# First DFT stage of batches 2 to 7: sums and differences of mirrored rows on GpSimd, 14 products of 120x120 in place of 16 of 94x96

## The chip, the cores and the metric

The kernel runs on one core of a Trainium2 chip. The metric is the device time of one execution in microseconds, the median of several runs. The engines are called TensorE (PE; PEld is its loading of weights), VectorE (DVE), ScalarE (ACT), GpSimd (POOL) and SyncE (SP), as the profile does.

## What is computed

An input x of shape (8, 3008, 256) is filtered along its sequence in the frequency domain, and the result goes through a feed-forward layer with a snake activation:

```python
X = np.fft.rfft(x, axis=1)
y = np.fft.irfft(X * (filt_r + 1j * filt_i)[None], n=3008, axis=1)
x = y.reshape(8 * 3008, 256)
h = x @ w_in                            # 256 -> 2048
g = h + np.sin(alpha * h) ** 2 / (alpha + 1e-09)
out = g @ w_out                         # 2048 -> 256
```

## The kernel before

The sequence of 3008 is split as 47 x 64: position t = 64 n1 + n2. The forward transform of a batch has a **first stage** over n1 (47 rows to 24 frequencies s, real and imaginary parts), a second stage over n2 with the twiddle factors in its tables, a product with the filter, and two stages back. The class `Spectral` holds a batch; batch 0 is done by code of its own before the main loop, and batch 1 shares its methods with batches 2 to 7.

- `load_x` (line 141) brings one of four chunks of x from DRAM as fp16, by a casting DMA that GpSimd issues: 94 partitions (47 n1 by two halves h of the 64 columns n2), 8 columns n2 of 256 channels each. For batches from 2 on it waits for the latest snake operation issued so far, which paces it.
- `first` (line 181) is the first stage: 16 matrix products per batch of the table `wf_t` (94x96) with two columns n2, so 512 columns on TensorE, into a PSUM tile `pa`. `evac` (lines 160 and 162) copies each to `t1_h`, two times in three on ACT and once on DVE. After every fourth product a DMA on SP stores the finished eight columns to `d1` in DRAM (line 186).
- `load_t2` (line 193, DMAs of GpSimd) reads `d1` back with n2 on the partitions. `forward` (line 201) is the second stage; its result `xf` is copied by ACT, and SP sends it back with its two halves exchanged as `xs` (line 208). `product` (line 215) and `cross` (lines 221 and 222) are three products or sums on DVE, each with both inputs in SBUF. `inverse` (line 232) and `last` (line 254) go back to `y` in SBUF.
- The feed-forward layer runs over 48 chunks of up to 512 tokens. `hidden` makes 16 blocks per chunk: two products into one of four PSUM buffers `ph` (line 540), the sine on ACT (`cos_all`, line 544), and one DVE operation that reads `cos_all` and `ph` and writes `v` (line 545), called the snake here. `project` (line 557) multiplies the chunk before by `w_out`.

The order of the work is written out by hand. The main loop counts **steps**, eight per chunk, 48 per batch; a step issues two `hidden` blocks and a part of `project`. `put(at, ...)` lists a piece of the spectral work with the step at which it is due, and `slot` issues what is due between them, at most one piece on TensorE at a time. With z = 48 b for batch b, its x is loaded from z - 92 on, the first stage starts at z - 67, `load_t2` is due at z - 56, the second stage runs from z - 46.8 and the last stage ends in the steps after z. Batch 2 has due times of its own: loads at steps 22, 27, 32 and 37, the first stage from step 36. So the first stage of a batch overlaps with the filter products of the batch before. All engines execute their instructions in the order in which they were issued. PSUM tiles `pa`, `pb`, `pc` and `pd` share two buffers; x has four buffers.

Of the kernel before, what the change touches and what calls it, by code (L numbers as in the profile page):

```python
# [18 lines left out]
B, S, C = 8, 3008, 256  # L19
DFF = 2048  # L20
N1, N2 = 47, 64
NS, NQ = 24, 64
NR = 2 * N1
NK = 4 * NS
FUSED = 1


def dft_tables():

    n1, n2 = np.arange(N1), np.arange(N2)  # L30
    s, q = np.arange(NS), np.arange(NQ)
    ph = 2 * np.pi * np.outer(n1, s) / N1
    w = np.stack([np.cos(ph), -np.sin(ph)], 1)
    wf = np.zeros((N1, 2, 2, NS, 2))
    wi = np.zeros((2, NS, 2, N1, 2))
    v = np.stack([2 * np.cos(ph), -2 * np.sin(ph)], 0)
    v[0, :, 0], v[1, :, 0] = 1.0, 0.0
    for h in range(2):
        wf[:, h, :, :, h] = w
        wi[:, :, h, :, h] = v.transpose(0, 2, 1) * (8.0 / S)  # L40

    kap = np.where(q[:, None] < 32, s + N1 * q[:, None], s + N1 * (95 - q[:, None]))
# [12 lines left out]
    wi0[:, :, :NS] = wi.transpose(0, 2, 1, 3)  # L55
    d = d.reshape(128, NS, 128).astype(f16)
    e = d.transpose(2, 1, 0) * f16(0.125)
    return (wf.reshape(NR, NK).astype(f16), wi.reshape(NK, NR).astype(f16), d,
            wf0.reshape(96, 128).astype(f16), wi0.reshape(128, NR).astype(f16), e)


# [1 line left out]
def kernel(  # L63
# [8 lines left out]
    out: bass.AP,  # L72
):
    nc = tc.nc
    wf_host, wi_host, d_host, wf0_host, wi0_host, e_host = dft_tables()
    wf_dram = nc.inline_tensor(wf_host, name="wf_tbl")
    wi_dram = nc.inline_tensor(wi_host, name="wi_tbl")
    d_dram = nc.inline_tensor(d_host, name="d_tbl")
    wf0_dram = nc.inline_tensor(wf0_host, name="wf0_tbl")
    wi0_dram = nc.inline_tensor(wi0_host, name="wi0_tbl")  # L80
# [6 lines left out]
    def after(ins, other):  # L87

        tc.add_manual_dep(ins.ins, other.ins.name, mybir.DependencyInfo(
            mybir.DependencyClass.Sync, mybir.DependencyReason.DATA), reason="order of loads")  # L90

    def pool(name, bufs, space=None):
        kw = {} if space is None else {"space": space}
        return ctx.enter_context(tc.tile_pool(name=name, bufs=bufs, **kw))

    cpool = pool("consts", 1)
    xpool = pool("xp", 4)
    t2pool = pool("t2", 4)
    xfpool = pool("xf", 3)
    ppool = pool("pp", 4)  # L100
# [4 lines left out]
    dpool = pool("dram", 2, DRAM)  # L105
    fps = pool("fps", 2, PSUM)
# [1 line left out]
    ops = pool("ops", 2, PSUM)  # L108

    wf_t = cpool.tile([NR, NK], FP16)  # L110
    t1_h = [cpool.tile([128, 16, C], FP16, name=f"t1_h{i}") for i in range(2)]
    t4_a = cpool.tile([128, 2, 16, C], FP16)
    t4_h = [t4_a[:, i] for i in range(2)]

    def by_half(t):

        return t.rearrange("p a (b c) -> p (a b) c", c=128)

    cos_all = cpool.tile([128, 4, 512], FP32)
    y = cpool.tile([128, 2, 2, 32, NR], FP16)  # L120
# [15 lines left out]
    marks = {}  # L136

    def load_x(b, ch):
        xt = xpool.tile([NR, 8, C], FP16, name=f"x_{b}_{ch}", tag="x")
        for n0, n in [(0, 8)] if b or ch < 3 else [(0, 4), (4, 4)]:  # L140
            ins = nc.gpsimd.dma_start(  # L141
                out=xt[:, n0:n0 + n],
                in_=bass.AP(tensor=x.tensor, offset=x.offset + (b * S + ch * 8 + n0) * C,
                            ap=[[32 * C, NR], [C, n], [1, C]]),
            )
# [11 lines left out]
    def evac(dst, src, on_act=None):  # L157
        flip[0] = (flip[0] + 1) % 3
        if flip[0] if on_act is None else on_act:
            marks["act"] = nc.scalar.copy(out=dst, in_=src)  # L160
        else:
            marks["dve"] = nc.vector.tensor_copy(out=dst, in_=src)  # L162

    class Spectral:

        def __init__(self, b):
            self.b = b
            self.d1 = dpool.tile([2 * NS, N2, C], FP16, name=f"d1_{b}", tag="d1")
            self.d2 = dpool.tile([2 * NS, N2, C], FP16, name=f"d2_{b}", tag="d2")
            self.d1_rows = self.d1.rearrange("a (h n) c -> (a h) n c", h=2)  # L170
            self.d2_rows = self.d2.rearrange("a (h n) c -> (a h) n c", h=2)
            self.x, self.t2, self.t4, self.xf, self.xs, self.p = {}, {}, {}, {}, {}, {}
            self.fused = b >= FUSED

        def load_x(self, ch):
# [2 lines left out]
        def first(self, i):  # L178
            ch, j = divmod(i, 4)
            ps = fps.tile([128, 512], FP32, name=f"pa_{self.b}_{i}", tag="f")  # L180
            marks["pe"] = nc.tensor.matmul(out=ps[0:NK, :], lhsT=wf_t, rhs=self.x[ch][:, 2 * j:2 * j + 2, :],  # L181
                                           start=True, stop=True)
            r0 = 8 * (ch % 2)
            evac(t1_h[ch // 2][0:NK, r0 + 2 * j:r0 + 2 * j + 2, :], ps[0:NK, :])
            if j == 3:
                nc.sync.dma_start(out=self.d1_rows[:, 8 * ch:8 * ch + 8, :], 
                                  in_=t1_h[ch // 2][0:NK, r0:r0 + 8, :])

        def load_t2(self, g):
            self.t2[g] = t2pool.tile([128, 6, C], FP16, name=f"t2_{self.b}_{g}", tag="t2")  # L190
# [73 lines left out]
    id32 = cpool.tile([16, 16], FP32)  # L264
    nc.scalar.dma_start(out=id32, in_=id32_dram.ap())

    x0 = [xpool.tile([NR, 8, C], FP16, name="x_0_0", tag="x")] + [load_x(0, ch) for ch in range(1, 4)]
    nc.gpsimd.dma_start(out=d_t, in_=d_dram.ap())
    id16 = cpool.tile([128, 128], FP16)
    nc.gpsimd.dma_start(out=id16, in_=id16_dram.ap())  # L270
# [25 lines left out]
    for g in range(2):  # L296
        gs = slice(12 * g, 12 * g + 12)
        for k, filt in enumerate((filt_r, filt_i)):
            for q in range(2):
                if (g, k, q) == (0, 1, 1):  # L300
# [3 lines left out]
                    out=f_t[k][64 * k + 32 * q:64 * k + 32 * q + 32, gs, :],  # L304
# [132 lines left out]

    def product_0(i):
        hc, w = blocks[i]
        p0[i] = xpool.tile([128, 2, 4, 128], FP16, name=f"p_0_{i}", tag="x")  # L440
        marks["products"] = nc.vector.tensor_tensor(
            out=p0[i].rearrange("p f s (k c) -> p f s k c", k=2),
            in0=xf0[i].rearrange("p s (k c) -> p s k c", k=2)[:, None].to_broadcast([128, 2, 4, 2, 64]),
            in1=filt_t[:, :, 4 * w:4 * w + 4].rearrange("p f s (k c) -> p f s k c", k=2)[..., 64 * hc:64 * hc + 64],
            op=ALU.mult)
# [24 lines left out]
            after(ins, marks["filt", 1, 1])  # L470
    nc.sync.dma_start(out=wf_t, in_=wf_dram.ap())
    nc.sync.dma_start(out=wi_t, in_=wi_dram.ap())
    w_out32 = vpool.tile([128, 16, C], FP32, name="w_out32", tag="v")
    for jb in range(0, 16, 8):
        ins = nc.sync.dma_start(out=w_out32[:, jb:jb + 8],
# [117 lines left out]
    def put(at, fn, *args, pe=False):  # L593
        pending.append((at, len(pending), pe, fn, args))
# [14 lines left out]
    for b in range(1, B):  # L609
        s = s1 if b == 1 else Spectral(b)  # L610
        z = 48 * b
        if b > 1:
            for ch in range(4):
                put((22,27,32,37)[ch] if b == 2 else z - 92 + 7 * ch, s.load_x, ch)
        for i in range(16):
            put(7.9 + 0.3 * i if b == 1 else 36 + 0.66 * i if b == 2 else z - 67 + 0.66 * i, s.first, i, pe=True)
        for g in range(4):
            put(12.5 if b == 1 else max(z - 56, 46.5), s.load_t2, g)
        for u in range(12):
            inv = 23.5 + 1.25 * u if b == 1 else 59 + 2.1 * u if b == 2 else z - 40.8 + 2.3 * u  # L620
# [69 lines left out]
```

## Time and profile before

| | |
|---|---|
| Time, median of 3 runs | 787.67 us (787.63 to 788.89) |
| Profiled execution, first to last instruction (span) | 786.7 us; the median of the runs lies 1.0 us above it |
| TensorE (PE) busy | 773.5 us, 98%, 5799 products |
| DVE busy | 657.6 us, 84% |
| ACT busy | 616.5 us, 78% |
| GpSimd (POOL) busy | 79.5 us, 10% |
| Granted TensorE clock | 1.000 |
| DMA | 100.99 MB, 128 GB/s on average |

In the profile, a group of instructions stands as line, engine, operation, output<-inputs with partitions x elements, count, then its busy time and the mean length of one, and last the idle time of the engine ahead of it with what ended it. A timeline row gives the start in us, the length in us, the engine and the instructions merged into that row. A product on TensorE has a modelled end that overlaps the next one's start, so distances from start to start tell its price. The run has one profiled execution; the page gives its span, and the time outside it is what the median has above it.

### The profile page before, as it was taken

How to read it: one execution, taken by the hardware profiler on the slowest of the kernel's cores; microseconds unless marked ns; L12 is line 12 of the kernel's file. 1: busy time of each engine (PE TensorE's matmuls, PEld its weight loads, DVE VectorE, ACT ScalarE, POOL GpSimd, SP SyncE). 2: the span in 40 equal slices, each digit the busy share in tenths (PEclk: the TensorE clock that was granted, in tenths of full speed). 3: DMA queues.
4: the chain of work that ended last, by engine and by line, in shares of the span. 5: the costliest groups of instructions: out<-in, count | busy, mean ns of one | idle time of the engine just before them, and what ended most of it. 6: DMA issues, size and time to landing. Idle time of an engine off the chain costs nothing.

```text
span 786.7 us, 16619 instructions
## 1 busy us (share of the span) xinstructions
PE 773.5 (98%) x5799; PEld 535.0 (68%) x5799; DVE 657.6 (84%) x1172; ACT 616.5 (78%) x1208; POOL 79.5 (10%) x125
## 2 busy tenths in 40 slices
PE   8998999999999999999999999999999999999998
PEld 4756766666667766777666766777666776766666
DVE  7887997899878997799977998799987999777773
ACT  5797878888878887888877888788887887777674
POOL 6442000200020000200020000200002000000000
PEclk9999999999999999999999999999999999999999
DMA  9965568665473646554575454845556243421111
GB/s 213 258 131 157 113 145 223 153 123 133 134 198 84 134 99 195 143 120 110 120 200 128 103 106 139 224 87 113 129 155 181 61 99 81 117 62 28 41 41 54
DMA packets 87692, 100.99 MB, mean 128 GB/s; under 512 B 14488, under 2 KB 75944, under 8 KB 87608
## 3 DMA queue, kind: packets, MB, share of 16 engines
q1 hardware_dynamic: 78032, 73.73, 34.5%
q0 software_dynamic: 9360, 26.15, 17.7%
q8 instruction: 45, 0.74, 0.4%
q14 instruction: 39, 0.32, 0.1%
q10 hardware_dynamic: 216, 0.05, 0.0%
HBM read 55.72 MB, written 46.66 MB: 130 GB/s over the span
## 4 chain that ended last, share of the span: by engine, by line
PE 89%; DVE 5%; ACT 2%; DMA 2%; issue 1%; SPq 1%; ACTq 0%; DVEq 0%
PE po L557 39%; PE ph L540 38%; PE pa L181 3%; PE pd L254 2%; DVE v L545 2%; PE pb L201 2%; PE pc L232 2%; DMA xs<-xf 1%; ACT cos_all L544 1%; DMA al<-in_moe_alpha_dram 1%; PE warm L381 1%; PE pc L453 0%; SPq L585 0%; ACT t_h L160 0%; DVE filt_t L162 0%
## 5 line engine op out<-in xcount | busy, mean ns | idle before, releaser
L545 DVE SCALAR_TENSOR_TENSOR v<-cos_all,ph 128x512 f16<-128x512 f32 (+1 forms) x768 | 483.0, 672 | 108.1 <-ACT cos_all L544 104.8
L544 ACT ACTIVATE cos_all<-ph 128x512 f32<-128x512 f32 (+1 forms) x768 | 411.1, 592 | 93.9 <-PE ph L540 92.9
L540 PE MATMUL ph<-y,w 128*128 128x512 f16 (+1 forms) x1536 | 388.4, 374 | 1.7 <-DVE y L162 0.9
L557 PE MATMUL po<-w,v 128*128 128x256 f16 x3008 | 389.5, 272 | 0.0
L557 PEld LDWEIGHTS <-v 128*128 128x128 f16 x3008 | 288.3, 98 | 77.7 <-issue 1.4
L540 PEld LDWEIGHTS <-w 128*128 128x128 f16 x1536 | 147.9, 98 | 106.5 <-issue 6.1
L565 ACT COPY o<-po 128x512 f32<-128x512 f32 (+1 forms) x97 | 55.6, 574 | 20.2 <-PE po L557 12.9
L204 ACT CAST xf<-pb 128x512 f16<-128x512 f32 x84 | 50.0, 595 | 16.4 <-PE pb L201 12.7
L193 POOL DMA_DIRECT2D t<-d x56 | 36.4, 669 | 204.6 <-DMA out_dram<-o 99.8
L160 ACT CAST t_h<-pa 96x512 f16<-96x512 f32 x74 | 43.3, 585 | 10.6 <-PE pa L181 10.5
L141 POOL DMA_DIRECT2D x<-in_x_dram x32 | 17.1, 536 | 298.2 <-PE pc L232 171.2
L160 ACT CAST y<-pd 128x376 f16<-128x376 f32 (+1 forms) x82 | 39.5, 482 | 8.8 <-PE pd L254 5.3
L254 PEld LDWEIGHTS <-t_a 96*128 96x128 f16 x448 | 31.3, 97 | 18.7 <-issue 0.4
L181 PE MATMUL pa<-x,wf_t 94*96 94x512 f16 x112 | 42.3, 381 | 1.6 <-ACT t_h L160 1.3
L160 ACT CAST g<-pc 128x512 f16<-128x512 f32 x58 | 34.4, 593 | 8.0 <-PE pc L232 7.7
L222 DVE TENSOR_TENSOR p<-p,xs 128x512 f16<-128x512 f16 x84 | 35.7, 425 | 2.9
L254 PE MATMUL pd<-wi_t,t_a 96*128 96x94 f16 x448 | 37.1, 204 | 0.0
L221 DVE TENSOR_TENSOR xs<-xs,filt_t 128x512 f16<-128x512 f16 x84 | 35.2, 420 | 0.8 <-DMA xs<-xf 0.8
L215 DVE TENSOR_TENSOR p<-xf,filt_t 128x512 f16<-128x512 f16 x84 | 35.2, 419 | 0.0
L232 PE MATMUL pc<-p,e_t 128*128 128x256 f16 x168 | 32.1, 273 | 0.8 <-ACT xf L204 0.5
L201 PE MATMUL pb<-t,d_t 128*128 128x256 f16 x168 | 32.1, 272 | 0.2
L162 DVE CAST y<-pd 128x376 f16<-128x376 f32 (+2 forms) x46 | 24.9, 544 | 1.5 <-PE pd L343 1.0
(66 smaller groups left out, 264.4 us busy)
## 6 DMA issues: line engine op xcount, KB each, us to landing
x<-in_x_dram POOLq DMA_DIRECT2D x30, 376.0 KB, 4.9
d<-t_h SPq DMA_DIRECT2D x28, 384.0 KB
t<-d POOLq DMA_DIRECT2D x56, 192.0 KB, 4.6
xs<-xf SPq DMA_DIRECT2D x168, 64.0 KB
d<-g SPq DMA_DIRECT2D x56, 192.0 KB
t_a<-d SPq DMA_DIRECT2D x28, 384.0 KB
out_dram<-o SPq DMA_DIRECT2D x104, 80.0 KB
w_out<-in_moe_w_out_dram SPq DMA_DIRECT2D x2, 1024.0 KB
```

The lines of the kernel that those rows point to most:

```text
L160: marks["act"] = nc.scalar.copy(out=dst, in_=src)
L181: marks["pe"] = nc.tensor.matmul(out=ps[0:NK, :], lhsT=wf_t, rhs=self.x[ch][:, 2 * j:2 * j + 2, :], start=True, stop=True)
L193: nc.gpsimd.dma_start(out=self.t2[g][64 * p:64 * p + 64, :, :], in_=self.d1[a0:a0 + 6, :, :].rearrange("s n c -> n s c"))
L201: nc.tensor.matmul(out=ps[:, i, :], lhsT=d_t[:, s, :], rhs=self.t2[s // 6][:, s % 6, :], start=True, stop=True)
L204: nc.scalar.copy(out=self.xf[u], in_=ps)
L232: nc.tensor.matmul(out=ps[:, i, :], lhsT=e_t[:, 2 * w + i, :], rhs=pt[:, i, :], start=(k == 0), stop=(k == len(pr) - 1))
L254: nc.tensor.matmul(out=psv[:, i, :], rhs=wi_t, start=True, stop=True, lhsT=t4_h[ch // 2][0:NK, n0 % 16 + i, cb * 128:cb * 128 + 128])
L540: nc.tensor.matmul(out=ps[:, 0:n], lhsT=w1[:, cb, jb * 128:jb * 128 + 128], rhs=y_cols[:, cb, c0:c0 + n], start=(cb == 0), stop=(cb == 1))
L544: nc.scalar.activation(out=cs[:, 0:n], in_=ps[:, 0:n], func=AFT.Sin, bias=float(np.pi / 2))
L545: marks["snake"] = nc.vector.scalar_tensor_tensor(out=v[k][:, jb, 0:n], in0=cs[:, 0:n], scalar=-1.0, in1=ps[:, 0:n], op0=ALU.add, op1=ALU. ...
L557: nc.tensor.matmul(out=pso[k][:, t % 2, :], lhsT=v[k][:, jb, 128 * t:128 * t + 128], rhs=w2[:, jb, :], start=(jb == 0), stop=(jb == 15))
L565: nc.scalar.copy(out=o[:, i0:t % 2 + 1, :], in_=pso[k][:, i0:t % 2 + 1, :])
```

## The change

For batches 2 to 7 the first stage uses the symmetry of cosine and sine. For n1 = 1 to 23 the row n1 and its mirror 47 - n1 share the cosine and have opposite sines. GpSimd adds and subtracts the two rows (`fold`), and the sums are multiplied by the cosine table, the differences by the sine table: 24 rows in place of 47. The freed rows carry five groups j of 13 columns, n2 = 13 j + l - 1 with l from 0 to 12, which makes 65 columns, the first of them unused. So a product has 5 x 24 = 120 rows and 120 results, and takes two values of l: seven values of i, two products each, 12 of 512 columns and 2 of 256 per batch. The last two share one PSUM tile and one evacuation, so there are 13 evacuations in place of 16.

The rows come by three DMAs per batch instead of four: 115 rows of 13 columns for n1 = 1 to 23, five rows for n1 = 0, and 115 mirrored rows, read from DRAM in a pattern of 5 by 23 rows of 13 KB. They go to `mirror[0]` and `mirror[1]`, which together with two of the four buffers of sums lie in the space of the four x buffers (`x_all`); the other two lie in unused columns of `t1_a`. `start_folding` clears `mirror[1]` once, so that n1 = 0 has a mirror of zeros. The stores to `d1` remain four per batch, two after i = 3 (8 columns) and two after i = 6 (5 columns), each of 120 partitions. One more table, `wp_t`, is loaded at the start on SP.

In due times: the loads at z - 92 and z - 83 (batch 2: steps 22 and 31), fold i at z - 70.4 + 1.4 i (batch 2: 32.6 + 1.4 i), its two products at z - 67 + 1.4 i and 0.7 later (batch 2: 36 + 1.4 i). GpSimd does not wait for these steps as such: a fold runs when its rows have landed and its sum buffer is free. The clearing is due at step 21.

```diff
+FOLDED = 2
+NJ, NL = 5, 13
+NF = NJ * NS
...
+    even = np.cos(ph[:NS])
+    odd = -np.sin(ph[:NS])
+    wp = np.einsum("kis,jm->jiksm", np.stack([even, odd]), np.eye(NJ))
+    wp = np.concatenate([wp[:, 1:].reshape(NF - NJ, 2, NF), wp[:, 0].reshape(NJ, 2, NF)])
...
-    t1_h = [cpool.tile([128, 16, C], FP16, name=f"t1_h{i}") for i in range(2)]
+    t1_a = cpool.tile([128, 2, 16, C], FP16)
+    t1_h = [t1_a[:, i] for i in range(2)]
+    wp_t = cpool.tile([NF, 2, NF], FP16)
...
+    x_all = cpool.tile([128, 4, 8, C], FP16)
...
+    STORES = {3: 0, 6: 8}
+    NP = (NL + 1) // 2
+    x_rows = x_all.rearrange("p a n c -> p (a n) c")
+    mirror = [x_rows[:, 16 * k:16 * k + NL, :] for k in range(2)]
+    sums = [t[0:NF, NL:NL + 2, :] for t in (t1_h[0], t1_h[1], x_rows[:, 0:16], x_rows[:, 16:32])]
+
+    def start_folding():
+
+        nc.gpsimd.memset(mirror[1].bitcast(UINT32), 0)
...
+            if self.folded:
+                self.d1_all = dpool.tile([2 * NS, NJ * NL, C], FP16, name=f"d1_{b}", tag="d1f")
+                self.d1 = self.d1_all[:, 1:1 + N2, :]
+                self.d1_fold = self.d1_all.rearrange("(k s) (j l) c -> k (s j) l c", k=2, j=NJ)
...
+        def load_mirror(self, k):
+            rows = [mirror[k][0:NF - NJ]] + ([] if k else [mirror[k][NF - NJ:NF]])
+            for at, t in zip((N2 * (N1 - 1) if k else N2, 0), rows):
+                ins = nc.gpsimd.dma_start(
+                    out=t, in_=bass.AP(tensor=x.tensor, offset=x.offset + (self.b * S + at - 1) * C,
+                                       ap=[[NL * C, NJ], [-N2 * C if k else N2 * C, NS - 1 if at else 1],
+                                           [1, NL * C]]))
+                after(ins, marks["snake"])
+
+        def fold(self, i):
+            l0, n = 2 * i, min(2, NL - 2 * i)
+            xa, xb = [t[0:NF, l0:l0 + n, :] for t in mirror]
+            self.e[i] = sums[i % 4]
+            nc.gpsimd.tensor_tensor(out=self.e[i][:, 0:n, :], in0=xa, in1=xb, op=ALU.add)
+            nc.gpsimd.tensor_tensor(out=xa, in0=xa, in1=xb, op=ALU.subtract)
+
+        def first_folded(self, i, k):
+            l0, n = 2 * i, min(2, NL - 2 * i)
+            if n == 2 or k == 0:
+                self.ps1 = fps.tile([128, 2, C], FP32, name=f"pa_{self.b}_{i}_{k}", tag="f")
+            ps = self.ps1
+            if k == 0:
+                src = self.e[i][:, 0:n, :]
+            else:
+                src = mirror[0][0:NF, l0:l0 + n, :]
+            dst = ps[0:NF, 0:2, :] if n == 2 else ps[0:NF, k:k + 1, :]
+            nc.tensor.matmul(out=dst, lhsT=wp_t[:, k, :], rhs=src, start=True, stop=True)
+            if n == 2:
+                evac(t1_a[0:NF, k, l0:l0 + 2, :], ps[0:NF])
+            elif k == 1:
+                evac(t1_a[0:NF, :, l0, :], ps[0:NF])
+            if i in STORES and k == 1:
+                lo = STORES[i]
+                n = l0 + n - lo
+                for part in range(2):
+                    nc.sync.dma_start(out=self.d1_fold[part, :, lo:lo + n, :], in_=t1_a[0:NF, part, lo:lo + n, :])
...
+    nc.sync.dma_start(out=wp_t, in_=wp_dram.ap())
...
-        if b > 1:
-            for ch in range(4):
-                put((22,27,32,37)[ch] if b == 2 else z - 92 + 7 * ch, s.load_x, ch)
-        for i in range(16):
-            put(7.9 + 0.3 * i if b == 1 else 36 + 0.66 * i if b == 2 else z - 67 + 0.66 * i, s.first, i, pe=True)
+        if s.folded:
+            if b == FOLDED:
+                put(21, start_folding)
+            for k in range(2):
+                put((22 if b == 2 else z - 92) + 9 * k, s.load_mirror, k)
+            for i in range(NP):
+                at = (36 if b == 2 else z - 67) + 1.4 * i
+                put(at - 3.4, s.fold, i)
+                for k in range(2):
+                    put(at + 0.7 * k, s.first_folded, i, k, pe=True)
+        else:
+            for i in range(16):
+                put(7.9 + 0.3 * i, s.first, i, pe=True)
```

More of the change, by code (lines that the diff above doesn't have):

```diff
@@ L57, in dft_tables @@
     e = d.transpose(2, 1, 0) * f16(0.125)
-    return (wf.reshape(NR, NK).astype(f16), wi.reshape(NK, NR).astype(f16), d,
+    even = np.cos(ph[:NS])
+    odd = -np.sin(ph[:NS])
+    wp = np.einsum("kis,jm->jiksm", np.stack([even, odd]), np.eye(NJ))
+    wp = np.concatenate([wp[:, 1:].reshape(NF - NJ, 2, NF), wp[:, 0].reshape(NJ, 2, NF)])
+    return (wp.astype(f16), wf.reshape(NR, NK).astype(f16), wi.reshape(NK, NR).astype(f16), d,
             wf0.reshape(96, 128).astype(f16), wi0.reshape(128, NR).astype(f16), e)
@@ L74 @@
     nc = tc.nc
-    wf_host, wi_host, d_host, wf0_host, wi0_host, e_host = dft_tables()
+    wp_host, wf_host, wi_host, d_host, wf0_host, wi0_host, e_host = dft_tables()
     wf_dram = nc.inline_tensor(wf_host, name="wf_tbl")
     wi_dram = nc.inline_tensor(wi_host, name="wi_tbl")
+    wp_dram = nc.inline_tensor(wp_host, name="wp_tbl")
     d_dram = nc.inline_tensor(d_host, name="d_tbl")
@@ L96 @@
     cpool = pool("consts", 1)
-    xpool = pool("xp", 4)
     t2pool = pool("t2", 4)
@@ L117, in by_half, with x_tile @@
         return t.rearrange("p a (b c) -> p (a b) c", c=128)
+    x_all = cpool.tile([128, 4, 8, C], FP16)
+    x_made = []
+    def x_tile():
+        x_made.append(x_all[:, len(x_made) % 4])
+        return x_made[-1]
     cos_all = cpool.tile([128, 4, 512], FP32)
@@ L138, in load_x @@
     def load_x(b, ch):
-        xt = xpool.tile([NR, 8, C], FP16, name=f"x_{b}_{ch}", tag="x")
+        xt = x_tile()[0:NR]
         for n0, n in [(0, 8)] if b or ch < 3 else [(0, 4), (4, 4)]:
@@ L167, in __init__ @@
             self.b = b
-            self.d1 = dpool.tile([2 * NS, N2, C], FP16, name=f"d1_{b}", tag="d1")
+            self.folded = b >= FOLDED
+            if self.folded:
[3 more added lines that the diff above has]
+            else:
+                self.d1 = dpool.tile([2 * NS, N2, C], FP16, name=f"d1_{b}", tag="d1")
+                self.d1_rows = self.d1.rearrange("a (h n) c -> (a h) n c", h=2)
             self.d2 = dpool.tile([2 * NS, N2, C], FP16, name=f"d2_{b}", tag="d2")
-            self.d1_rows = self.d1.rearrange("a (h n) c -> (a h) n c", h=2)
             self.d2_rows = self.d2.rearrange("a (h n) c -> (a h) n c", h=2)
-            self.x, self.t2, self.t4, self.xf, self.xs, self.p = {}, {}, {}, {}, {}, {}
+            self.e, self.x, self.t2, self.t4, self.xf, self.xs, self.p = {}, {}, {}, {}, {}, {}, {}
             self.fused = b >= FUSED
@@ L265 @@
     nc.scalar.dma_start(out=id32, in_=id32_dram.ap())
-    x0 = [xpool.tile([NR, 8, C], FP16, name="x_0_0", tag="x")] + [load_x(0, ch) for ch in range(1, 4)]
+    x0 = [x_tile()[0:NR]] + [load_x(0, ch) for ch in range(1, 4)]
     nc.gpsimd.dma_start(out=d_t, in_=d_dram.ap())
@@ L439, in product_0 @@
         hc, w = blocks[i]
-        p0[i] = xpool.tile([128, 2, 4, 128], FP16, name=f"p_0_{i}", tag="x")
+        p0[i] = x_tile()[:, 0:4].rearrange("p n (f c) -> p (n f) c", f=2).rearrange("p (f s) c -> p f s c", f=2)
         marks["products"] = nc.vector.tensor_tensor(
@@ L611 @@
         z = 48 * b
-        if b > 1:
-            for ch in range(4):
-                put((22,27,32,37)[ch] if b == 2 else z - 92 + 7 * ch, s.load_x, ch)
-        for i in range(16):
-            put(7.9 + 0.3 * i if b == 1 else 36 + 0.66 * i if b == 2 else z - 67 + 0.66 * i, s.first, i, pe=True)
+        if s.folded:
[8 more added lines that the diff above has]
+                    put(at + 0.7 * k, s.first_folded, i, k, pe=True)
+        else:
+            for i in range(16):
+                put(7.9 + 0.3 * i, s.first, i, pe=True)
         for g in range(4):
```

## The prediction, made before the change was run

> **What bounds the kernel now.** I read the busy times on the page first, then the busy time by stretch, then the stretches of the engines' timelines around the first stage of batch 3, and last the waits of TensorE.
>
> From the page's first part and its groups:
>
> ```profile
> PE 773.5 (98%) x5799; PEld 535.0 (68%) x5799; DVE 657.6 (84%) x1172; ACT 616.5 (78%) x1208; POOL 79.5 (10%) x125
> ...
> L181 PE MATMUL pa<-x,wf_t 94*96 94x512 f16 x112 | 42.3, 381 | 1.6 <-ACT t_h L160 1.3
> ```
>
> TensorE is busy 98% of the span, GpSimd 10%. The 112 products of the first stage (batches 1 to 7, 16 each) wait for 1.6 us in all. The 381 ns of one are a length with modelled pipeline; the price on the path is the distance to the next start. The timeline of TensorE in batch 2 gives it:
>
> ```profile
> 116.89 0.38 PE L181 MATMUL pa<-x,wf_t 94*96 94x512 f16 x1
> 117.11 1.04 PE L557 MATMUL po<-w,v 128*128 128x256 f16 x8
> 117.99 0.38 PE L181 MATMUL pa<-x,wf_t 94*96 94x512 f16 x1
> 118.21 1.03 PE L540 MATMUL ph<-y,w 128*128 128x512 f16 x4
> ```
>
> A product of 512 columns moves the next start by 0.22 us (0.216 over many), whatever its rows. From about 160 us to the end the starts follow each other at that rate without a gap over 0.25 us, so TensorE's columns set the time there, and each wait put on it is paid in full. The busy time by stretch shows what stands close behind:
>
> ```profile
> 168.00:180.00 12.00, 12.00 (x96) 8.61 (x95) 11.64 (x24) 10.24 (x20) 0.51 (x1) 1.00 0.61 131
> 180.00:190.00 10.00, 10.00 (x72) 6.85 (x70) 9.82 (x20) 7.97 (x16) 0.51 (x1) 1.00 0.57 119
> ```
>
> The columns are PE, PEld, DVE, ACT, POOL, the clock and DMA. While batch 2 is in its forward products (and batch 3's x is loaded), DVE is busy for 21.46 of 22 us: it has 0.54 us to spare. How far DVE may fall behind before TensorE stops is read from both timelines:
>
> ```profile
> 175.14 1.28 DVE L545 SCALAR_TENSOR_TENSOR v<-cos_all,ph 128x512 f16<-128x512 f32 x2
> 176.33 0.42 DVE L221 TENSOR_TENSOR xs<-xs,filt_t 128x512 f16<-128x512 f16 x1
> 176.79 0.42 DVE L222 TENSOR_TENSOR p<-p,xs 128x512 f16<-128x512 f16 x1
> ```
>
> ```profile
> 177.69 1.03 PE L540 MATMUL ph<-y,w 128*128 128x512 f16 x4
> ```
>
> The hidden products have four PSUM buffers, so the pair starting at 177.69 reuses those that the pair of snakes at 175.14 frees. The second of them ends at 176.42 and its buffer is written again at 177.69 + 0.43: **1.7 us of slack** for DVE.
>
> **Part by part.** *Products.* Per batch 16 x 512 columns become 12 x 512 and 2 x 256, the work of 13: three fewer, 3 x 0.216 = 0.65 us, in six batches **-3.9 us**. All of it lies on the path. The weight load alternates between two tables, but every product has its own load already (5799 of both); the present one takes 123 ns under a product of 216 ns, and only the last pair of a batch, of 107 ns each, is shorter than its load, by 16 ns: 0.2 us over the run at most, taken as zero.
>
> *Evacuations.* 13 in place of 16 per batch (the last, half-width, pair shares one): about one less on DVE (0.6 us start to start) and two on ACT (585 ns each). Neither sets the end, so zero; they give DVE about 0.6 us of room in that stage. If TensorE waited for DVE there, they would be worth up to those 0.6 us per batch.
>
> *Folds.* 14 GpSimd operations of 120x512 f16 per batch. The nearest rows are GpSimd's own products, in the groups of that engine:
>
> ```profile
> L482 POOL TENSOR_TENSOR w<-w_in,y 128x768 f16<-128x768 f32 x4 | 7.2, 1824 | 12.1 <-DVE rec_t L358 12.1
> L482 POOL TENSOR_TENSOR w<-w_in,y 128x512 f16<-128x512 f32 x2 | 2.6, 1280 | 0.0
> ```
>
> I take 1.28 us each (1.09 us for the elements by the difference of the two rows, 0.19 fixed): 18 us per batch, on an engine that sits idle. Four sum buffers let folds 0 to 3 (8 operations, 10.2 us) run as soon as the rows have landed; folds 4 to 6 follow TensorE, each released by the product four folds before, 5.6 steps of some 2.1 us ahead of its use. So TensorE does not wait for a fold from batch 3 on. The memset of 128x1664 words at step 21, by the existing memsets (128 columns in 266 ns, 16 in 165) under 2 us, is covered by 12 us of idle GpSimd before the load of step 22. Queued behind the folds on GpSimd are only the t2 loads, due at z - 56, six steps after the last fold.
>
> *Loads.* Three DMAs replace four, for nearly the same bytes: 115 rows of 13 KB twice. From batch 3 on, the second goes out at z - 83 and is wanted at z - 67: 16 steps, over 30 us, cover it. In batch 2 it goes out at step 31 and the first product stands at step 36. GpSimd's timeline dates the steps:
>
> ```profile
> 96.00 0.54 POOL L141 DMA_DIRECT2D x<-in_x_dram  x1 [10.86 <-PE pc L232]
> 107.81 0.52 POOL L141 DMA_DIRECT2D x<-in_x_dram  x1 [11.27 <-DVE p L215]
> 118.30 0.52 POOL L141 DMA_DIRECT2D x<-in_x_dram  x1 [9.97 <-PE po L557]
> ```
>
> These are steps 27, 32 and 37, so step 31 is at 105.4. A load of 376 KB lands in 4.9 us (the page); one of 748 KB takes between that and twice it, 9.8; I take 7.4. It lands at 112.8, the first sum is there at 114.1, and TensorE wants it at 113.4 (its first pa): **+0.7 us**, between 0 and 3.1. If the rows go over fewer DMA engines it is more. In the trace's DMA records one row (8 KB read) holds its engine for 0.32 us; a row of 13 KB then holds it 0.52 us, and 23 rows on each of five engines take 12 us and land at about 119, +7 us. On this point the row is that the 94-row load lands in 4.9 us, so it is spread over all 16 engines. The Trainium skill (DMA: Bandwidth & Descriptors, "Why a DMA increments its semaphore by 16 and not by 1") lets the number of engines be the largest divisor up to 16 of the slowest dimension, which would be 2 for 94 rows, and allows an exception for some direct copies; the new source pattern of 5 by 23 would by that rule get 5.
>
> *Stores and SP.* Four stores per batch as before (120 partitions, 8 or 5 rows each), the last due 0.8 step earlier; each waits for an evacuation at SP's head, as now, with the xs exchanges behind it. The wp table adds one 0.35 us issue ahead of w_out, whose use on GpSimd comes after 9.65 us of weights_in. Zero for both; without cover the table would cost its 0.35 us.
>
> *DVE beside GpSimd.* This is the unknown. In the 10 us of the first burst (batch 3: about 170 to 180 us) DVE issues seven products with two SBUF inputs (L215, L221, L222), and five more while folds 4 to 6 run. The trace has no such product beside a GpSimd product. Its nearest row is the snakes beside the weight products that GpSimd makes from 30.5 to 47.5 us, in DVE's timeline:
>
> ```profile
> 38.12 4.88 DVE L545 SCALAR_TENSOR_TENSOR v<-cos_all,ph 128x512 f16<-128x512 f32 x8 [1.09 <-ACT cos_all L544]
> ```
>
> That is 0.61 us each, as elsewhere, but a snake reads one operand from SBUF and one from PSUM. So the wait per DVE product lies between 0 and a whole GpSimd operation, 1.28. For a likely value I take half of the element part, **0.55 us**, what is left on average of an operation that is met at random: it sits between the undisturbed row and the full length. First burst: 7 x 0.55 = 3.85 us, less 1.7 of slack and 0.5 of spare DVE time, leaves 1.65 on TensorE. Second stretch, GpSimd about 75% busy: 5 x 0.75 x 0.55 = 2.06, less 1.6 (0.4 of slack regained, 0.6 of idle DVE and 0.6 of the evacuation saved), leaves 0.46. So 2.1 us per batch. It strikes batches 3 to 7; batch 1's last DVE products end as batch 2's folds begin. Five times 2.1 is **+10.5 us**. The ends: nothing at 0; with 0.64 for the first of each and a whole 1.28 for the second of an L221-L222 pair, 5.8 - 2.2 and 3.4 - 1.6, 5.4 per batch, +27. The Trainium skill (SBUF — State Buffer, "Who interferes with whom") speaks against the change: a DVE instruction with two SBUF inputs and a GpSimd instruction that reads SBUF exclude each other, the second fully blocked until the first is done. By that rule the upper end, about 812, would hold; by the undisturbed snakes, about 784.5; no run here shows a two-input product under it yet.
>
> **The sum.** The profiled span is 786.7 us and the median of the runs 787.67; the 1.0 us outside the span stays. -3.9 + 0.7 + 10.5 = +7.3, so 787.7 + 7.3 = **795.0 us**.
>
> **Rivals.** *Free folds, faster.* GpSimd's reads leave DVE alone, or the wait stays under 0.4 us, where 2.8 + 1.5 us are nearly absorbed by the slack. For it: GpSimd 90% idle, snakes undisturbed. Against: DVE is 97% busy just there. Time 787.7 - 3.9 + 0.7 = 784.5; down to 783.8 with an early load. It decides from a wait of 0.40 us per DVE product, at which 0.6 us per batch, 3 us in all, pay back the gain. *About no change:* waits of 0.37 to 0.43 us, or the free case with 2 to 5 us lost in batch 2, 786.1 to 789.2. *Late load:* no contention, but batch 2's rows on five engines: -3.9 + 7 = +3.1, 790.8. For it: the two-level source pattern; against: the even spread of the 94 rows.
>
> **How the numbers follow.** Contention over 0.43 us: 0.52, own range 789.3 to 812. Late load alone: 0.08. About no change: 0.08. Free folds: 0.32. A measurement of this kernel can tell 0.2%, 1.6 us. So slower 0.60, same 0.08, faster 0.32. The range runs from 784.0, inside the free case, to 810.0, near the end of the contention: each side leaves out about one in ten.
>
> **What would show it.** Right: L215, L221 and L222 grow from 0.42 us to about 1 us, or stand further apart, where folds run; the hidden products (ph) then wait for L545 or evacuations for some 2 us in each of five batches; pa shows 84 products in batches 2 to 7 with 78 evacuations. Wrong: the DVE products keep 420 ns beside the folds; GpSimd operations far from 1.28 us; a landing of the loads of 13 KB rows over 10 us; or a wait of TensorE on a fold in batch 3 or later.

## The result and the profile after

The changed kernel takes 880.14 us (median of 4 runs, 877.4 to 884.33) against 788.28 us: 1.117 times the time before, 95% interval 1.114 to 1.120. The forecast was 795.0 us, at most 810. The direction was right, the size was not: 92 us in place of 7.

The page of the changed kernel, first the engines, then the granted clock by slice, then the groups that have changed (columns as before):

```profile
PE 793.5 (91%) x5787; PEld 539.7 (62%) x5787; DVE 681.5 (78%) x1166; ACT 613.7 (70%) x1196; POOL 175.2 (20%) x204
...
PEclk9999979989999989999999988999999999999999
...
L291 DVE TENSOR_TENSOR xs<-xs,filt_t 128x512 f16<-128x512 f16 x84 | 45.2, 538 | 69.1 <-DMA xs<-xf 67.8
L302 PE MATMUL pc<-p,e_t 128*128 128x256 f16 x168 | 33.9, 285 | 67.7 <-DVE p L292 61.5
...
x_all<-in_x_dram POOLq DMA_DIRECT2D x12, 747.5 KB, 15.5
```

TensorE is busy 91% of the span and not 98%. Its inverse products `pc` wait 61.5 us for DVE's L292, which is behind L291 (both are `cross`), and L291 waits 67.8 us for the DMA that brings the exchanged half `xs`. Before, L291 waited 0.8 us for it. The twelve loads of 748 KB land after 15.5 us (a load of 376 KB: 4.9). The line of the core gives the clock:

```profile
core 0: 875.6 us, clock 0.963
```

The profiled span grew by 88.9 us, from 786.7 to 875.6. Of this, 68.9 us are idle time of TensorE (82.1 in place of 13.2), most of it the waits of `pc`. The other 20.0 us are busy time (793.5 in place of 773.5), though there are fewer products. The missing 3.7% of the clock over 875.6 us would be 32.4 us, but part of the half speed falls into the waits, where it costs nothing more: by the clock records and TensorE's instructions 20.3 us of it were lost while TensorE worked.

One such stop, in batch 4's load, from the timelines of GpSimd, DVE, SP and TensorE:

```profile
289.45 0.68 POOL L225 DMA_DIRECT2D x_all<-in_x_dram  x1 [17.25 <-DVE v L616]
305.13 1.14 POOL L235 TENSOR_TENSOR t_a<-x_all 120x512 f16<-120x512 f16 x1 [15.00 <-DMA x_all<-in_x_dram]
```

```profile
306.49 1.29 DVE L291 TENSOR_TENSOR xs<-xs,filt_t 128x512 f16<-128x512 f16 x1 [8.89 <-DMA xs<-xf]
307.81 1.26 DVE L292 TENSOR_TENSOR p<-p,xs 128x512 f16<-128x512 f16 x1
```

```profile
296.44 2.09 SPq L278 DMA_DIRECT2D xs<-xf  x2
298.63 8.06 SPq L656 DMA_DIRECT2D out_dram<-o  x7
```

```profile
298.42 1.03 PE L611 MATMUL ph<-y,w 128*128 128x512 f16 x4
309.13 0.61 PE L302 MATMUL pc<-p,e_t 128*128 128x256 f16 x2 [9.69 <-DVE p L292]
309.53 1.92 PE L628 MATMUL po<-w,v 128*128 128x256 f16 x8
...
313.20 1.04 PE L628 MATMUL po<-w,v 128*128 128x256 f16 x8
```

The load goes out at 289.45 and has landed when the first fold starts at 305.13. The exchange issued at 296.44 lands only after it: DVE stands idle for 8.89 us. SP needs 8.06 us to get seven output stores out (seven in a row take 2.59 to 4.85 us in the trace of before). Each issue takes 0.27 to 0.50 us; in the rest of the time SP waits for earlier transfers to land, whose semaphores (the counters that tell of a landing) these stores use again. The same wait stands ahead of the exchanges, in the changed kernel and then in the one before:

```profile
SPq L278 <- DMA out_dram<-o: 24.5, 12, 4.1
```

```profile
SPq L208 <- DMA out_dram<-o: 0.7, 1, 0.7
```

The columns of such a line are us in total, times, and the longest. After 9.69 us of standstill TensorE starts again at half speed: eight `po` products take 1.92 us in place of 1.04. The clock records have half speed from 302.5 to 312.7 us, so it began 3.0 us into the stop and lasted for 3.6 us of work. And in the same place the two DVE products take 1.29 and 1.26 us in place of 0.42: the folds, which started at 305.13, hold them off.

In the trace's DMA records the 115 rows of this load take 0.51 us each, and the sum of their times over the stretch that they fill is 4.8 engines. So the load does go over five of the sixteen. The records name no engine, but the landings show the five: each DMA counts its semaphore up by sixteen. Of the exchange issued at 296.44, eleven counts came by 298.42 and the last five from 305.72 to 306.22, after the load's last row had ended at 304.60; of its other half, eleven by 299.97 and five from 305.89 to 306.39. Over the run 42 of the 168 such DMAs had counts later than 4 us after their issue, and in 39 of these it was five counts.

### The profile page after: what moved, and what is told of

The parts are those of the page before. It is cut to its first block, busy times and chain, and to the rows that moved or that the text cites. A ratio compares the mean times of both kernels' runs of the same rounds, so it can differ in the third digit from the quotient of the medians.

```text
span 875.6 us, 16638 instructions
## 1 busy us (share of the span) xinstructions
PE 793.5 (91%) x5787; PEld 539.7 (62%) x5787; DVE 681.5 (78%) x1166; ACT 613.7 (70%) x1196; POOL 175.2 (20%) x204
## 4 chain that ended last, share of the span: by engine, by line
PE 65%; DMA 18%; DVE 10%; ACT 3%; issue 2%; SPq 2%; ACTq 0%; DVEq 0%
PE po L628 28%; PE ph L611 28%; DMA xs<-xf 15%; DVE v L616 4%; DMA out_dram<-o 3%; DVE p L292 2%; PE pc L302 2%; DVE xs L291 2%; ACT cos_all L615 2%; PE pd L324 2%; PE pb L271 1%; PE pa L248 1%; SPq L656 1%; PE pc L523 1%; DMA cos_all<-in_x_dram 1%
## 5 line engine op out<-in xcount | busy, mean ns | idle before, releaser
L628 PE MATMUL po<-w,v 128*128 128x256 f16 x3008 | 398.4, 276 | 0.0
L611 PE MATMUL ph<-y,w 128*128 128x512 f16 (+1 forms) x1536 | 396.3, 380 | 2.3 <-DVE v L616 1.2
L628 PEld LDWEIGHTS <-v 128*128 128x128 f16 x3008 | 293.2, 99 | 81.5 <-issue 0.9
L291 DVE TENSOR_TENSOR xs<-xs,filt_t 128x512 f16<-128x512 f16 x84 | 45.2, 538 | 69.1 <-DMA xs<-xf 67.8
L302 PE MATMUL pc<-p,e_t 128*128 128x256 f16 x168 | 33.9, 285 | 67.7 <-DVE p L292 61.5
L177 ACT CAST g<-pc 128x512 f16<-128x512 f32 x57 | 33.7, 591 | 61.5 <-PE pc L302 61.1
L302 PEld LDWEIGHTS <-e_t 128*128 128x128 f16 x168 | 14.7, 99 | 82.5 <-DVE p L292 68.1
L235 POOL TENSOR_TENSOR t_a<-x_all 120x512 f16<-120x512 f16 x24 | 29.0, 1207 | 165.6 <-PE pa L248 76.4
L292 DVE TENSOR_TENSOR p<-p,xs 128x512 f16<-128x512 f16 x84 | 50.8, 604 | 2.9
L225 POOL DMA_DIRECT2D x_all<-in_x_dram x18 | 11.5, 641 | 198.8 <-DVE v L616 114.6
L236 POOL TENSOR_TENSOR x_all<-x_all 120x512 f16<-120x512 f16 (+1 forms) x42 | 47.7, 1136 | 3.3
L324 PEld LDWEIGHTS <-t_a 96*128 96x128 f16 x448 | 31.8, 98 | 18.3 <-issue 0.2
L177 ACT CAST t_a<-pa 120x512 f16<-120x512 f32 (+1 forms) x62 | 36.7, 593 | 6.8 <-PE pa L248 4.0
## 6 DMA issues: line engine op xcount, KB each, us to landing
x_all<-in_x_dram POOLq DMA_DIRECT2D x12, 747.5 KB, 15.5
```

Of the source, the lines that this page charges most:

```text
L236: nc.gpsimd.tensor_tensor(out=xa, in0=xa, in1=xb, op=ALU.subtract)
L291: nc.vector.tensor_tensor(out=xs, in0=xs, in1=f_t[1][:, 2 * u:2 * u + 2, :], op=ALU.mult)
L292: nc.vector.tensor_tensor(out=p, in0=p, in1=xs, op=ALU.add)
L302: nc.tensor.matmul(out=ps[:, i, :], lhsT=e_t[:, 2 * w + i, :], rhs=pt[:, i, :], start=(k == 0), stop=(k == len(pr) - 1))
L324: nc.tensor.matmul(out=psv[:, i, :], rhs=wi_t, start=True, stop=True, lhsT=t4_h[ch // 2][0:NK, n0 % 16 + i, cb * 128:cb * 128 + 128])
L611: nc.tensor.matmul(out=ps[:, 0:n], lhsT=w1[:, cb, jb * 128:jb * 128 + 128], rhs=y_cols[:, cb, c0:c0 + n], start=(cb == 0), stop=(cb == 1))
```

## The experiments

Times are medians; "before" was run beside each group on the same chip, with medians of 788.4 to 789.0 us. The groups ran on different chips. A line further down in a kernel can have moved by one to three: L292 of the changed kernel is L293 or L294 where the program is longer.

**First group: loads and folds apart.**

The loads in three DMAs:

```diff
+BLOCKS = [(0, 1), (1, 8), (9, 8), (17, 7)]
...
-            for at, t in zip((N2 * (N1 - 1) if k else N2, 0), rows):
+            for i0, n in BLOCKS[k:]:
```

> The change as it is, but each load of 115 rows is cut into three DMAs of 5 by 8, 5 by 8 and 5 by 7 rows (the table's rows are reordered to match); bytes and folds are unchanged. Theory (few DMA engines): a load of 5 by 23 rows goes over five DMA engines for 13.4 us, the xs exchanges that use the same engines land late, DVE's L291 and then TensorE's inverse products wait (61.5 us), and the granted clock halves after each stop (about 32 us). If three DMAs go over different engines, a group of rows lands in 6 to 9 us, the waits of L291 on xs fall from 67.8 to under 15 us and the time to 785 to 805. Rival (folds): GpSimd's folds block DVE's two-input products, and these are what TensorE waits for: the time stays at 865 to 885.

The change without the loads of batches 3 to 7:

```diff
-                put((22 if b == 2 else z - 92) + 9 * k, s.load_mirror, k)
+                if b == FOLDED:
+                    put(22 + 9 * k, s.load_mirror, k)
```

> The change with the loads of batches 3 to 7 left out: their folds work on what is left in the buffers (the difference is taken the other way round, so that values stay bounded), so the results of these batches are not the reference's. Folds, products, stores and order are unchanged. Theory (few DMA engines): only batch 2's two loads remain, of about 15 us of stops with their clock loss; 795 to 810. Rival (folds): 860 to 885.

The change without the folds:

```diff
-                src = self.e[i][:, 0:n, :]
+                src = mirror[1][0:NF, l0:l0 + n, :]
...
-                put(at - 3.4, s.fold, i)
```

> The change without the folds: the products read the loaded rows themselves, not their sums and differences, so the spectral part is not the reference's. Loads, products and stores are unchanged. Theory (few DMA engines): 855 to 885. Rival (folds): 783 to 790.

Both edits at once, the loads in three DMAs of 5 by 8 or 7 rows and no folds:

> Both at once: loads cut into three DMAs and no folds (results not the reference's, as without folds). Both theories: what the three products fewer per batch are worth when nothing disturbs, 783.5 to 787. The first kernel of this call less this one is the price of the folds: theory 2 to 20 us, rival 80 us.

Measured:

| loads | with folds | without folds |
|---|---|---|
| 5 by 23 rows (the change) | 880.1 | 861.8 (ratio 1.093, 1.089 to 1.098) |
| three DMAs | 825.9 (1.046, 1.045 to 1.048) | 802.3 (1.018, 1.016 to 1.019) |
| none after batch 2 | 807.9 (1.025, 1.023 to 1.027) | not run |

Without folds the change loses only 18 us of its 92: the rival, that the folds do it all, falls. With the loads in three DMAs it loses 54. DVE's wait for xs goes with the loads and not with the folds, here without folds and then with the loads in three DMAs (the change: 67.8 us):

```profile
DVE xs L291 <- DMA xs<-xf: 68.1, 15, 9.0
```

```profile
DVE xs L292 <- DMA xs<-xf: 20.2, 10, 3.6
```

The waits of TensorE on L292 in the four kernels, in the order of the list above:

```profile
PE pc L303 <- DVE p L293: 20.7, 19, 3.4
```

```profile
PE pc L302 <- DVE p L292: 13.6, 7, 11.4
```

```profile
PE pc L302 <- DVE p L292: 47.6, 13, 7.6
```

```profile
PE pc L303 <- DVE p L293: 7.3, 7, 2.7
```

The kernel without later loads keeps one long stop, of 11.4 us, in batch 2. Its profiled span is 20.7 us longer than before: TensorE is idle for 18.6 us more and busy for 2.1 us more. It does not give the price of the folds, since without loads to wait for they run earlier: in batches 3 to 7 the first eight run mostly ahead of the DVE products that they would meet. The kernels without later loads and without folds came out in the ranges that the theory expected. The two kernels with cut loads came out above: 825.9 where 785 to 805 was expected, and 802.3 where 783.5 to 787 was. By the DMA records the three DMAs together held about ten engines for 7 to 9 us, and still DVE waited for xs, 20.2 us where under 15 was expected. So cut loads still did harm, and the folds cost 23.6 us where 2 to 20 was expected.

**Second group: when the loads run, and the folds.** In this group and the next the clearing is due at step 13, ahead of the earlier loads of batch 2.

```diff
-                put((22 if b == 2 else z - 92) + 9 * k, s.load_mirror, k)
+                for g in range(3):
+                    put((14 if b == 2 else z - 92) + 9 * k + 3 * g, s.load_mirror, k, g)
```

without folds:

> Three DMAs per load as before, but each due three steps (some 6 us) after the one ahead (z - 92 to z - 77; batch 2 from step 14), so that no two are in flight at once; no folds, so results are not the reference's. With all three at once 802.3 was measured. Theory (length of the burst on the engines that carry xs): each DMA holds five engines for 4 us only; the waits of L291 on xs fall from 19.7 to under 5 us; 783.5 to 790. Rival (long rows: a row of 13 KB holds an engine 0.51 us and delays an exchange whenever it comes): 798 to 806.

and with them:

> The same spaced loads with the folds, so the whole change with other loads. Less the kernel without folds this is the price of the folds alone, undisturbed by late exchanges. Theory (folds block DVE's two-input products, as predicted): 8 to 25 us above it. Rival (the 18 to 24 us between the kernels with and without folds came from the loads' delays acting on a DVE that was already late): 0 to 5 us above it.

The loads as in the change, but early:

```diff
-                put((22 if b == 2 else z - 92) + 9 * k, s.load_mirror, k)
+                put((13.2 if b == 2 else z - 103) + 1.5 * k, s.load_mirror, k)
```

> The change with its loads of 5 by 23 rows as they are, but due at z - 103 and z - 101.5 (batch 2: 13.2 and 14.7), in the gap between the exchanges of two batches; folds 0 to 3 then run as soon as the rows land, mostly before the DVE products of the batch ahead begin. Theory (a load costs where an exchange is in flight, a fold where a two-input DVE product is): the exchanges start at z - 94.8, some 17 us after the first load; 785 to 805. Rival (five-engine loads or folds cost wherever they stand): 860 to 885.

The same due times with the loads in three DMAs and two more sum buffers:

```diff
+    sums += [x_rows[0:NF, 15:32:16, :], t1_a[0:NF, :, 15, :]]
...
-            self.e[i] = sums[i % 4]
+            self.e[i] = sums[i % 6]
```

> Loads cut in three, at z - 103 and z - 101.5, and six sum buffers in place of four (the two more lie in unused rows), so that folds 0 to 5 run early and only the short fold 6 follows TensorE. Theory: neither loads nor folds meet an exchange or a DVE product for long; the three products fewer are what is left: 783.5 to 790. Rival (cost wherever they stand): 815 to 830, as with the loads cut alone.

Spaced loads without folds took 804.2 us (1.021, 1.019 to 1.024): apart or together, the three DMAs cost about the same (802.3). That is in the range of this run's rival, long rows; taking the DMAs apart did not help. With folds it was 823.9 (1.045, 1.043 to 1.047), 19.7 us more, as the theory had it (8 to 25).

The two early kernels took 847.5 (1.074, 1.072 to 1.077) and 830.4 us (1.053, 1.052 to 1.055), and both missed. They were flawed: z - 103 of batch 3 lies ahead of batch 2's products, so batch 3's rows overwrote batch 2's (batch 2's results are not the reference's there), and TensorE stood for them, 18.5 and 10.5 us at once. For the later batches the loads queue on GpSimd behind the t2 loads and land when the exchanges have begun. Even so DVE's waits for xs fell, to 14.8 us with the loads whole (the change: 67.8) and 3.5 with the loads in three DMAs (20.2 at the old steps); TensorE's waits for L292 were 20.7 us in both, with the folds still beside the DVE products. A load that truly misses all exchanges was not tried.

**Third group: short rows, and the folds moved.** Each load in six DMAs, by three groups of rows and two halves of the columns (7 and 6 KB in place of 13), one about every two steps:

```diff
-                                ap=[[NL * C, NJ], [-N2 * C if k else N2 * C, n], [1, NL * C]]))
+                                ap=[[NL * C, NJ], [-N2 * C if k else N2 * C, n], [1, m * C]]))
...
+                put(13.5 + 1.6 * i if b == 2 else z - 92 + 1.9 * i, s.load_mirror, *piece)
```

without folds:

> Loads cut into twelve DMAs per batch, 5 by 8 (or 7) rows of 7 or 6 columns, each about two steps after the one ahead; no folds (results not the reference's). A row then holds its engine for about 0.28 us and a DMA is over in some 2 us, against 0.51 and 4 us in the kernel with three DMAs per load, which measured 804. Theory (an exchange waits for the rows ahead of it on its engine): the waits of L291 on xs fall under 5 us and the time to 784 to 790. Rival (something else than loads holds these kernels 15 us or more above the gain, such as the new stores or the order of the products): 798 to 806.

with folds as in the change:

> The same twelve DMAs, with the folds as in the change. Less the kernel without folds it is the price of the folds alone. Theory (a fold holds off a DVE product with two SBUF inputs for up to its whole length): 12 to 25 us above. Rival (folds cost only where exchanges are late): under 5 us above.

with folds that wait for their step, later:

```diff
-                put(at - 3.4, s.fold, i)
+                put((37 if b == 2 else z - 65) + 1.15 * i, s.fold, i)
...
+            after(ins, marks["snake"])
```

> The same twelve DMAs; fold i waits for the snake of step z - 65 + 1.15 i and the products follow from z - 63.5 (batch 2: 37 and 38.5), so that the folds run in the gap between the last DVE product of the batch ahead (z - 65) and the first of their own (z - 45); t2 loads at z - 55.5. Theory: folds meet no two-input DVE product, so L285, L291 and L292 stay within 20 ns of 420 on average and the time is that without folds, 784 to 790. Rival (folds slow the snakes, evacuations or TensorE itself, wherever they stand): as with the folds in their old place, 800 to 826.

Without folds: **786.7 us, 0.997 (0.996 to 0.999)**, 2.2 us under before and in the range expected. The dozen pieces do no harm that can be seen. In the DMA records one of their rows takes 0.29 or 0.25 us (median), less than the 0.32 of the four loads before. Added up, the rows of a batch are under way for longer than the long ones, 197 us in place of 156, so it is not that less stood in the way. Each DMA is half as large, too, and no run separates this from the shorter rows. Nor is the delay gone. From issue to the last count an exchange takes 2.0 us without a load beside it (median). Beside one it takes 8.1 us in the change (up to 14.5), 5.1 with the spaced long rows (up to 7.1) and 4.5 here (up to 6.3), which is in time for most. DVE's wait for xs in this kernel, and in the one with the spaced long rows:

```profile
DVE xs L292 <- DMA xs<-xf: 3.1, 5, 1.2
```

```profile
DVE xs L292 <- DMA xs<-xf: 17.5, 16, 3.6
```

With the folds in their place the same kernel takes 817.7 (1.036, 1.034 to 1.037): **the folds cost 31.0 us**, above the 12 to 25 expected, while DVE waits for xs only 4.7 us. Its timelines of DVE and GpSimd show how:

```profile
295.14 1.37 DVE L292 TENSOR_TENSOR xs<-xs,filt_t 128x512 f16<-128x512 f16 x1
296.55 1.26 DVE L293 TENSOR_TENSOR p<-p,xs 128x512 f16<-128x512 f16 x1
297.73 2.47 DVE L617 SCALAR_TENSOR_TENSOR v<-cos_all,ph 128x512 f16<-128x512 f32 x4
```

```profile
295.00 1.23 POOL L237 TENSOR_TENSOR x_all<-x_all 120x512 f16<-120x512 f16 x1
296.19 1.33 POOL L236 TENSOR_TENSOR t_a<-x_all 120x512 f16<-120x512 f16 x1
297.60 1.22 POOL L237 TENSOR_TENSOR x_all<-x_all 120x512 f16<-120x512 f16 x1
```

DVE's product of 295.14 ends at 296.51, 0.28 us after GpSimd's fold of 295.00; the next one, of 296.55, ends at 297.81, 0.29 us after the fold of 296.19. They alternate. In the whole run 43 of these products start while a fold is under way, and nearly all of them end 0.28 us after that fold; none of the products that meet no fold takes over 0.43 us. The snakes between them run beside folds at 0.6 us as ever. Over the run, the 252 DVE products with two SBUF inputs take 32.5 us more than before (mean 550 in place of 421 ns), and TensorE waits for their results and for the evacuations behind them:

```profile
PE pc L303 <- DVE p L293: 15.4, 11, 2.3
PE pc L303 <- DVE t_a L180: 8.7, 4, 2.9
```

With the folds moved behind the last DVE products the kernel takes 795.85 us (1.009, 1.007 to 1.010): 21.8 of the 31.0 us are back, and the DVE products exceed their old time by 4.6 us in place of 32.5. The rival, that folds harm as much wherever they stand, falls; the expected 784 to 790 was missed, with 9.1 us left.

**Fourth group: the 9 us that were left.**

```diff
-                put((37 if b == 2 else z - 65) + 1.15 * i, s.fold, i)
+                put((38 if b == 2 else z - 62.8) + 1.1 * i, s.fold, i)
```

> The kernel with twelve DMAs and late folds (795.9), with folds from z - 62.8 + 1.1 i and products from z - 61.3 (batch 2: 38 and 39.6), t2 loads at z - 53.5. Theory (what is left of its 9 us over the kernel without folds are the first folds, which still meet the last L292 of the batch ahead, whose mean was 474 ns): L292 falls under 440 ns and the time to 786 to 792. Rival (the later first stage itself costs, because stores, t2 loads and the second stage now follow each other too closely): 796 or more, with TensorE waiting on t2.

```diff
-FOLDED = 2
+FOLDED = 3
```

> The same, with batch 2 left on the old first stage (16 products, four loads of 94 rows), so that the folded stage holds for batches 3 to 7 only. It gives up 0.65 us of TensorE's columns. Theory (batch 2 stands in the closest part of the schedule, with exchanges every 1.25 steps and 4.8 us of gaps between 100 and 120 us): 784.5 to 789, under the kernel with batch 2 folded. Rival (batch 2 costs no more than the others): 0.5 to 2 us above it.

L222 is L294 here. Its group in the kernel with the folds from z - 65, and then in these two, where it is the same:

```profile
L294 DVE TENSOR_TENSOR p<-p,xs 128x512 f16<-128x512 f16 x84 | 39.8, 474 | 2.9
```

```profile
L294 DVE TENSOR_TENSOR p<-p,xs 128x512 f16<-128x512 f16 x84 | 36.5, 435 | 2.9
```

The move freed the DVE products (0.7 us over, in the run), but the time hardly moved: 794.95 us (1.008, 1.006 to 1.010), where 786 to 792 was expected. The first fold's meeting with L294 was not the rest. With batch 2 left on the old stage: **790.4 us, 1.002 (1.001 to 1.003)**, so about 4.6 us of it stood in batch 2, as expected, though the range expected (784.5 to 789) was missed. In the kernel with batch 2 folded, TensorE waits there for t2, which is now loaded later:

```profile
PE pb L273 <- DMA t<-d: 2.4, 1, 2.4
```

What holds the last version 3.7 us above the kernel with small loads and no folds is not settled; its profile shows many waits of 0.2 to 0.9 us around the later first stage, none of them large. No version with the folds beats the kernel before.

## Why the prediction was right or wrong

**The gain was about right.** Three products fewer per batch were put at 3.9 us. The kernel with short pieces and no folds gains 2.2 of them (1.1 to 3.2 by its interval), and its TensorE is busy for 770.1 us in place of 773.5.

**The step that failed most is *Loads*.** It put the loads at +0.7. Measured, they cost 75.1 us: 861.8 with the loads of the change and no folds, against 786.7 with small loads and no folds. The step asked whether the load would be there in time, found 30 us of cover from batch 3 on, took 7.4 us for the landing, and priced five engines only for batch 2, at +7. The landing took 15.5 us, and the DMA records show 4.8 engines. The Trainium skill (DMA: Bandwidth & Descriptors, "Why a DMA increments its semaphore by 16 and not by 1") lets such a DMA go over the largest number of engines up to 16 that divides the slowest dimension of both its sides. For 5 groups of rows and 115 partitions that is five; the prediction had worked this out and set it aside, and the trace agrees with it. What the step left out is who else uses the engines. The xs exchange of 64 KB is wanted 4.5 steps after it is sent, and it, the stores and SP's next issues came late while five engines were held by rows of 13 KB. The prediction's late load, put at 790.8, is the kernel without the folds, which measured 861.8. Its profiled span is 74.5 us longer than before: TensorE is idle for 55.3 us more, 47.6 of it the waits of `pc` on L292, and busy for 19.2 us more, by the slow clock. The cover of a transfer is not only its own due date but that of each transfer beside it.

**The clock was missing altogether.** No step priced what a stop of TensorE does afterwards. In the clock records of the changed kernel eleven stretches inside the run stand at half speed, of 3.4, 6.8 or 10.2 us each and 65 us in all. Some 24 us of them lie inside the waits; the other 41 cost half their length, 20.3 us, a third of the 61.5 us of waits. The Trainium skill (TensorE: Matmul & The Clock Gate, "Why this matters for your kernels") says that an idle gap of more than about 3 us brings the half clock. Here every stop of 3.0 us or more was followed by it, or fell into a stretch of it, but shorter ones could be as well: in the kernel with small loads and folds one of 2.04 us was, and one of 2.88 us was not. The trace of before showed none of it, since its clock was 1.000.

**Contention: the mechanism was right, the slack was not.** The folds were put at +10.5. They cost 31.0 us where nothing else held DVE up (18.3 on top of the late loads of the change). Predicted were 3.85 + 2.06 = 5.9 us of delay per batch on DVE's two-input products. Measured are 32.5 us in six batches, 5.4 per batch. That the two agree is in part luck: 42 products grew, seven per batch where twelve were counted, but by 0.78 us each and not by 0.55 or less. Batch 1's products, which the prediction left out, were held up as well, by 4.7 us. The alternation agrees with the exclusive lock that the Trainium skill describes (SBUF — State Buffer, "Who interferes with whom"), seen here as products of 1.26 to 1.37 us beside folds of 1.2. But 2.2 + 1.6 of the 5.9 were taken off as slack, which left 2.1 per batch, 10.5 in all. The slack of 1.7 us was read at the `ph` buffers. The first to need the delayed work is another: the inverse product that reads L222's output. In the trace of before, L222 ends 0.08 to 2.7 us ahead of that product's start in batches 2 to 7, and in 29 of the 72 pairs less than 0.5 us. The L222 of 176.79, which the prediction shows, ends at 177.21, and its product follows here:

```profile
177.47 0.38 PE L232 MATMUL pc<-p,e_t 128*128 128x256 f16 x2
```

That is 0.26 us, and it stood in the same window as the line that the 1.7 was read from.

**Of the signs named beforehand**, the longer L215, L221 and L222 came, the landing over 10 us (named as a sign of error) came, and the waits of TensorE stood at `pc` and not at `ph`. GpSimd's folds were priced well: 1.28 us predicted, 1.2 measured.

## What to carry to other kernels

Ask of a new transfer how many DMA engines it will hold and for how long per row, and then which short transfers on a deadline run in that time; cutting it into twelve small DMAs with short rows, as here 13 KB into 7 and 6, undid almost all of its harm here, by leaving each exchange late by less than it could bear. Put GpSimd's two-input work where DVE has no products with two SBUF inputs, and read DVE's slack at the first consumer of just those products, not at the buffer with the most room. On a TensorE that is full, price a stop twice: the wait, and the slow clock behind it.

## What the runs showed of the hardware that was not expected

- A load of 5 by 23 rows went over five DMA engines (4.7 to 5.1 on average, 13.4 to 14.5 us), one of 94 rows over most of the sixteen (11 to 14, about 3 us).
- While the five engines were held, SP took 8.06 us to issue seven stores that take 2.59 to 4.85 us otherwise: it waited for earlier transfers of its queue to land. Eleven of an exchange's sixteen landing counts came within 2 us of its issue, five only when the load was through.
- The half-speed stretches of TensorE's clock came in lengths of 3.4 us and its multiples up to 20.5 us, and a stop of 2.04 us could be enough to start one.
- A DVE product with two SBUF inputs that started during a GpSimd fold nearly always ended 0.28 us after the fold; a snake beside the folds kept its 0.6 us.
- Three DMAs of 13 KB rows, each after the other, did as much harm as all at once (804.2 against 802.3); twelve with rows half as long did none that could be seen.
